# Attention followed by two squared-ReLU MLPs on one core: second-layer weight units issued a unit behind, first products in three banks, sums before remainders

## Chip, cores and metric

The kernel runs on one core of a Trainium2 chip. The metric is the device time of one execution in microseconds (us), the median of several runs.

## The reference, cut to what matters

```python
x = attention(q, k, v)            # 4 x 8 heads x 576 x 64: 4 heads local, 4 strided; scale 1/8
x = x.transpose(0, 2, 1, 3).reshape(2304, 512)
for w_in, w_out in (moe, moe2):   # [512, 2048], [2048, 512]
    r = np.maximum(x @ w_in, 0.0)
    x = (r * r) @ w_out
```

The weights are float64: a weight arrives as two 32-bit words, and the kernel first makes a float32 value of them.

## The kernel before, in words

Every float32 product is split: an operand is kept as a high part (rounded to fp32r) and a remainder (value minus high part), and a product is three matmuls, high by high, high by remainder, remainder by high.

**Blocks and steps.** The 2304 tokens make five blocks in each layer. Layer 1 is blocks 0 to 4: blocks 0, 1, 2 and 4 have 512 tokens and 16 steps each, block 3 has 256 tokens and 8 steps, each step being one or two of the 16 pieces (128 columns) of the hidden dimension. Block 5 is the 256 tokens of layer 2, 8 steps. A step of the main loop (lines 1500 to 1542) issues `mm1` of the next step (line 966) and then `mm2` of its own (line 1014). `mm1` fills a PSUM tile `ps_h` (24 narrow or 12 wide matmuls); ScalarE then evacuates it in three instructions, `r` (line 1001, ReLU), `sq` (1006) and `gh` (1007), and VectorE makes the remainder `gl` (1011). `mm2` of the step needs `gh` and `gl`. Blocks 6 to 9 (the other 2048 tokens of layer 2) use a seven-product scheme, one `frame` (line 1265) for each pair of pieces, 8 pairs per block.

**Banks of the first product.** `mm1` takes its tile from the pool `ps_h` (one bank), except that line 974 chooses `ps_a` (three banks) when `n_att[0] == len(att)`. The list `att` of attention work ends with entries that hold no operation; `att_to` is never called beyond `att_end[-1]`, the end of the last entry that holds one, so `n_att[0]` stays below `len(att)`.

**Second-layer weights.** While blocks 3 to 5 run, the weights of layer 2 are prepared in a list of units, `conv2` (lines 428 to 436), nine for a pair of pieces and 144 in all. There are eight pairs of the outer weights first, then eight pairs of the inner weights. In every step there are eight places (`point`, line 1508), three inside `mm1`, one behind its evacuation, four in and behind `mm2`; each adds `PACE` = 0.65 to a credit, and each whole credit issues one unit. They begin at the first step of block 3. The order of one pair i is: `start2(i)`, `sums_3(i-2)`, `start2(i+1)`, `whole2(i)`, `whole2(i+1)`, `rest2(i)`, `rest2(i+1)`, `sums_1(i)`, `sums_2(i)`.

- `start2`: two VectorE instructions on the raw words (lines 242, 246), then a ScalarE scaling of the result (263).
- `whole2`: VectorE joins the words (268), then ScalarE writes the high part (362).
- `rest2`: VectorE subtracts (371). For outer weights the second `rest2` of a pair stores both pieces, 1 MB, to DRAM (374).
- `sums_1`, `sums_2`: four VectorE sums of halves (382), then ScalarE writes their high parts in one instruction (414). For outer weights the target is `ops_out(4, 4)`, one buffer for all pairs.
- `sums_3`: VectorE subtracts the remainders (382); for outer weights a load of the next piece and a 1 MB store of that buffer follow (423).

All DMAs are issued from one queue (SP), and each engine executes its instructions in the order in which they are issued.

**A frame.** TensorE fills `ps_m` by `visit` (line 1220) with two products; ScalarE copies it to `m` (line 1308, shown in the trace as tile `u`); VectorE adds the halves of `m` (`u2`, line 1315) and, after the next `visit`, `a11` (line 1323, tile `r`). Before `m` stands, on ScalarE, the copy `ah` of sums `s13` that VectorE makes at the head of the frame (1297); behind it stands `bh` (1310). VectorE makes `bl` (1311), `u2`, and `work[0]` (a sum for x of the next block, line 1317), in that order, ahead of `a11`. In the first frame of blocks 7, 8 and 9 four sums of the block before (`heads`) come ahead of `s13`. In the last frame of a block `early` (a copy and a remainder of x) comes ahead of `m`. The second `visit` of the frame may write the bank only when `a11` has read it. Between the visits stand `gaps`, products of the current pair.

Of the kernel before, what the change touches and what calls it, by code (L numbers as in the profile page):

```python
# [14 lines left out]
ALU = mybir.AluOpType  # L15
# [40 lines left out]
SHIFT = (0, 4, 0)  # L56


XALL = 6 * 4 * 512 + 80
AT_V, AT_XN = P + 2 * P + 126, P + 2 * P + 126 + 5 * 260  # L60
OTHERS = AT_XN + 256 + 64

PACE = 0.65
N_WARM = 8
ZEROS = (0, 0, 0, 0, 0, 2, 2, 2, 2, 4, 4, 4)

# [103 lines left out]
def tile_attention_then_two_mlps(  # L170
# [69 lines left out]
    def sign_and_end(n):  # L240
        lower, upper = words(n)
        nc.vector.tensor_scalar(
            out=lower, in0=lower, scalar1=29, scalar2=None, op0=ALU.logical_shift_right
        )
        if n >= N_SIGNS:
            nc.vector.scalar_tensor_tensor(  # L246
                out=lower, in0=upper, scalar=-(2 ** 31), in1=lower, op0=ALU.bitwise_and, op1=ALU.bitwise_or
            )
# [102 lines left out]
        else:  # L351
            w_nat[i] = ops_out(f % 2 * 2, 2)

    def start2(i):
        sign_and_end(half1 + i)
        exponent_range(half1 + i)

    def whole2(i):
        together(half1 + i)
        natural(i)  # L360
        v = val[half1 + i].rearrange("p (h m) -> p h m", h=2)
        nc.scalar.activation(out=w_nat[i][:, :, 0], in_=v, func=AF.Copy)
        if i < NF and i % 2 == 0:
            load2("out")

    done2 = set()

# [31 lines left out]
    def sums_2(i):  # L399
        s = s_sum[i]  # L400
        v0, v1 = values_of(i)
        if i < NF:
            tt(s[:, 1], v1[:, 1], s[:, 0], ALU.subtract)
            tt(s[:, 3], s[:, 1], v1[:, 0], ALU.subtract)
            w = ops_out(4, 4)
            s_parts[i] = w[:, :, 0], w[:, :, 1]
        else:
            tt(s[:, 1], s[:, 0], v0[:, 0], ALU.subtract)
            tt(s[:, 3], v0[:, 1], s[:, 1], ALU.subtract)
            s_parts[i] = [  # L410
                wpool.tile([P, 4, HALF], F32R, tag=slot("out", i % NF + a), name="s")
                for a in range(2)
            ]
        nc.scalar.activation(out=s_parts[i][0], in_=s, func=AF.Copy)
        for n in (i, i + 1):
            del val[half1 + n]

    def sums_3(i):
        h, lo = s_parts[i]
        tt(lo, s_sum.pop(i), r32(h), ALU.subtract)  # L420
        if i < NF:
# [3 lines left out]
                in_=r32(xall[:, units_at + 4 * U:units_at + 8 * U]),  # L425
            )

    conv2 = []
    for i in range(0, half2 + 2, 2):
        if i < half2:  # L430
            conv2.append((start2, i))
        if i:
            conv2.append((sums_3, i - 2))
        if i < half2:
            conv2 += [(start2, i + 1), (whole2, i), (whole2, i + 1), (rest2, i), (rest2, i + 1)]
            conv2 += [(sums_1, i), (sums_2, i)]

    def conv2_by(n):
        while n and n_conv2[0] < len(conv2):
            fn, i = conv2[n_conv2[0]]  # L440
            kind, _, f = piece2(i)
            if f >= n_load2[kind]:
                return
            fn(i)
            n_conv2[0] += 1
            n -= 1

# [518 lines left out]
    def mm1(s, point):  # L966

        if s >= len(steps):
            return
        k, f = steps[s]  # L970
        ne = tiles_of(k)
        n = TB // ne
        x_hi, x_lo = block_x(k)
        if s != 1 and n_att[0] == len(att):
            ps = ps_a.tile([P, TB], F32, tag="a", name="ps_h")
        elif s != 1:
            ps = ps_h.tile([P, TB], F32, tag="h", name="ps_h")
        else:
            ps = ps_a.tile([P, TB], F32, tag="a", name="ps_h")
        for c in range(KC):  # L980
            for e in range(ne):
                w = ready2(f + e) if k == NB else ready(("in", 0, f + e))
                for i, (a, x) in enumerate(((0, x_hi), (0, x_lo), (1, x_hi))):

                    last = c == KC - 1 and i == 2 and e == ne - 1
                    product(
                        ps[:, e * n:(e + 1) * n],
                        lhsT=w[:, c // 2, a, c % 2 * P:(c % 2 + 1) * P] if k == NB
                        else w[:, a, c * P:(c + 1) * P],
                        rhs=x[:, c] if k == NB else x[:, c, x_at(n):x_at(n) + n],  # L990
                        start=c == 0 and e == 0 and i == 0,
                        stop=last,
                        halves=last and k == NB - 1 and f == 0,
                    )
                    one_small()
            if c < KC - 1:
                point()
        g0 = 48 if ne > 1 and blocks[k][0] == 0 else 0
        r = gpool.tile([P, TB], F32, tag="r", name="r", bufs=1)
        sq = gpool.tile([P, TB], F32, tag="sq", name="sq", bufs=1)  # L1000
        nc.scalar.activation(out=r, in_=ps, func=AF.Relu, scale=W_BACK)  # L1001
        h = gpool.tile([P, TB + P], F32R, tag="gh", name="gh", bufs=2)[:, g0:g0 + TB]
        lo = gpool.tile([P, 3 * HALF], F32R, tag="gl", name="gl", bufs=2)[:, g0:g0 + TB]
        if 0 < n_load[0] - n_part[0] or 0 < n_conv2[0] < len(conv2):

            nc.scalar.activation(out=sq, in_=r, func=AF.Square)
            nc.scalar.activation(out=h, in_=sq, func=AF.Copy)  # L1007
        else:
            nc.scalar.activation(out=h, in_=r, func=AF.Square)
            nc.vector.tensor_tensor(out=sq, in0=r, in1=r, op=ALU.mult)  # L1010
        nc.vector.tensor_tensor(out=lo, in0=sq, in1=r32(h), op=ALU.subtract)  # L1011
        gh[s], gl[s] = h, lo
# [252 lines left out]
    def frame(gaps, nxt, cur, heads=(), copy=None, early=None, work=None, late=()):  # L1265
# [16 lines left out]
        if cur:  # L1282
            s13, s24 = (
                gpool.tile([P, TB + P], F32, tag="gh", name="s", bufs=2)[:, :TB].rearrange(
                    "p (i n) -> p i n", i=2)
                for _ in range(2)
            )
            nc.scalar.activation(out=ah[:, 2], in_=a12, func=AF.Copy)
            if heads:
                for one in heads[:2]:  # L1290
                    one()
                tt(al[:, 2], a12, r32(ah[:, 2]), ALU.subtract)
                for one in heads[2:]:
                    one()
            tt(s13[:, 0], a21, a22, ALU.add)
            tt(s13[:, 1], a11, a21, ALU.subtract)
            nc.scalar.activation(out=ah[:, 0:2], in_=s13, func=AF.Copy)  # L1297
            if not heads:
                tt(al[:, 2], a12, r32(ah[:, 2]), ALU.subtract)
            tt(s24[:, 0], s13[:, 0], a11, ALU.subtract)  # L1300
            tt(s24[:, 1], a12, s24[:, 0], ALU.subtract)
            tt(al[:, 0:2], s13, r32(ah[:, 0:2]), ALU.subtract)
        if early is not None:
            early()
        ps = ps_h.tile([P, TB], F32, tag="h", name="ps_m")
        visit(k, q, ps, ("11", 0), ("s2", 1))
        m, u = (vpool.tile([P, 512], F32, tag="val", name="u") for _ in range(2))
        nc.scalar.activation(out=m, in_=ps, func=AF.Copy, scale=W_BACK)  # L1308
        if cur:
            nc.scalar.activation(out=bh[:, 2:4], in_=s24, func=AF.Copy)  # L1310
            tt(bl[:, 2:4], s24, r32(bh[:, 2:4]), ALU.subtract)

        u2, u3 = m[:, HT:], u[:, HT:]
        u4 = u[:, :HT]
        tt(u2, m[:, :HT], m[:, HT:], ALU.add)
        if work is not None:
            work[0]()
        for one in gaps[0]:
            one()
        if copy is not None:  # L1320
            copy()
        visit(k, q, ps, ("12", 2))
        add(a11, ps[:, :HT], m[:, :HT])
        nc.scalar.activation(out=a11, in_=a11, func=AF.Relu)
        nc.scalar.activation(out=a11, in_=a11, func=AF.Square)
        parts(bh[:, 0], bl[:, 0], a11)
# [149 lines left out]
    with tc.manual_schedule():  # L1476
# [23 lines left out]
        for s in range(len(steps)):  # L1500
# [7 lines left out]
            def point(s=s, layer=layer, j=j, f=f):  # L1508
                n_pt[0] += 1
                at = N_PT * s + n_pt[0]  # L1510
                for b, (p0, p1) in enumerate(spans):
                    if at > p0:
                        lo, hi = att_end[b], att_end[b + 1]
                        if b == 0 and at < LATE * N_PT:
                            hi = lo + (hi - lo) * EARLY // 100
                            p1 = LATE * N_PT
                        elif b == 0:
                            lo += (hi - lo) * EARLY // 100
                            p0 = LATE * N_PT
                        att_to(min(hi, lo + -(-(hi - lo) * (at - p0) // (p1 - p0))))  # L1520
                if n_part[0] < half1:
                    conv_by(1)
                elif k >= NB - 2:
                    credit[0] += PACE
                    while credit[0] >= 1.0:
                        conv2_by(1)
                        credit[0] -= 1.0
# [53 lines left out]
```

## Time and profile before

| | |
|---|---|
| median of 3 runs | 970.28 us (968.94 to 971.01) |
| the profiled execution | 971.93 us |
| its span, first to last instruction | 970.2 us |
| TensorE matmul busy | 892.5 us, 92% |
| VectorE busy | 688.2 us, 71% |
| ScalarE busy | 524.7 us, 54% |
| GpSimd busy | 17.7 us, 2% |
| granted clock of TensorE, mean | 0.984 |

The profile is that of one execution. Matmuls are pipelined and their ends are modelled, so TensorE busy at 92% does not mean that it works at its peak; what it waits for is read from its waits. Blocks 3 to 5 lie from about 367 us to 597 us of the span, the frames from about 600 us to the end.

### The profile page before, as it was taken

Reading aid. Unit: us, or ns where it says so; the run is one execution under the profiler, and the core shown is the slowest. Engines: PE = TensorE matmul, PEld = TensorE weight load, DVE = VectorE, ACT = ScalarE, POOL = GpSimd, SP = SyncE. Lnnn points to the kernel's source line nnn. Section 1 sums busy time; section 2 is a strip of 40 time slices with the busy share of each in tenths; the row PEclk is TensorE's granted clock in tenths of the full one; section 3 lists DMA queues with packets and bytes.
Section 4 is the critical chain, followed back from the end, with each engine's and each line's share of the span. In section 5 each row is a group of like instructions: output and inputs, shape, how many; then the busy total and the mean of one; then the engine's idle time right before and its main releaser. Section 6 shows DMA issues by size and latency. Waiting matters only on the chain. (4 is left out here: it accounts for less than half of the span.)

```text
span 970.2 us, 16096 instructions
## 1 busy us (share of the span) xinstructions
PE 892.5 (92%) x5719; PEld 791.9 (82%) x5719; DVE 688.2 (71%) x1742; ACT 524.7 (54%) x1204; POOL 17.7 (2%) x15
## 2 busy tenths in 40 slices
PE   9899999999999998877887879999899989998998
PEld 8788888887888888866666768988798889888998
DVE  6898974787677744665676665777767777777766
ACT  6877864676666644455555553444444444444442
POOL 0700000000000000000000000000000000000000
PEclk9999999999999999999999989999999999998999
DMA  8955411222222105676943264655665566555653
GB/s 266 347 176 194 147 40 68 87 73 80 86 76 63 54 1 191 232 251 243 338 133 105 87 254 163 199 171 160 184 212 173 153 217 189 160 164 165 193 177 128
DMA packets 81247, 155.21 MB, mean 160 GB/s; under 512 B 7440, under 2 KB 36240, under 8 KB 78096
## 3 DMA queue, kind: packets, MB, share of 16 engines
q1 hardware_dynamic: 81168, 154.19, 48.6%
q8 instruction: 45, 0.74, 0.3%
q14 instruction: 34, 0.28, 0.1%
HBM read 127.95 MB, written 26.21 MB: 159 GB/s over the span
## 5 line engine op out<-in xcount | busy, mean ns | idle before, releaser
L958 PE MATMUL ps_h<-xall,w 128*128 128x512 f32 (+1 forms) x1153 | 257.6, 368 | 38.6 <-ACT r L1001 38.6
L958 PEld LDWEIGHTS ps_h<-xall,w 128*128 128x128 f32 x1153 | 190.8, 195 | 71.8 <-ACT r L1001 45.4
L958 PE MATMUL ps_y<-gh,w 128*128 128x512 f32 (+1 forms) x640 | 156.4, 375 | 3.7 <-ACT o L1056 3.1
L958 PEld LDWEIGHTS ps_y<-gh,w 128*128 128x128 f32 x640 | 108.1, 188 | 21.1 <-ACT o L1056 3.5
L1226 PE MATMUL ps_m<-xall,s 128*128 128x256 f32 x768 | 111.0, 288 | 12.9 <-DVE r L1069 6.7
L1226 PEld LDWEIGHTS ps_m<-xall,s 128*128 128x128 f32 x768 | 97.5, 192 | 21.8 <-DVE r L1069 11.1
L1011 DVE TENSOR_TENSOR gl<-sq,gh 128x512 fp32r<-128x512 f32 x80 | 55.4, 692 | 67.7 <-ACT gh L1007 63.3
L1226 PE MATMUL ps_m<-xall,w 128*128 128x256 f32 x576 | 87.6, 289 | 10.5 <-ACT u L1308 10.1
L1253 PE MATMUL ps_y<-w,bh 128*128 128x256 f32 x496 | 94.6, 284 | 0.0
L1226 PEld LDWEIGHTS ps_m<-xall,w 128*128 128x128 f32 x576 | 75.1, 191 | 17.2 <-ACT u L1308 17.2
L958 PE MATMUL ps_y<-gl,w 128*128 128x512 f32 (+1 forms) x324 | 84.0, 370 | 0.0
L1001 ACT ACTIVATE r<-ps_h 128x512 f32<-128x512 f32 x80 | 47.2, 590 | 60.6 <-PE ps_h L958 52.0
L382 DVE TENSOR_TENSOR bl<-r,bh 128x256 fp32r<-128x256 f32 x64 | 27.2, 425 | 72.0 <-ACT bh L1065 44.4
L1253 PEld LDWEIGHTS ps_y<-w,bh 128*128 128x128 f32 x496 | 77.8, 193 | 0.0
L1253 PE MATMUL ps_y<-w,ah 128*128 128x256 f32 x372 | 72.0, 283 | 0.0
L1253 PE MATMUL ps_y<-w,bl 128*128 128x256 f32 x248 | 70.4, 284 | 0.0
L958 PEld LDWEIGHTS ps_y<-gl,w 128*128 128x128 f32 x324 | 55.8, 188 | 9.6 <-DVE gl L1011 0.4
L1010 DVE TENSOR_TENSOR sq<-r 128x512 f32<-128x512 f32 x38 | 26.3, 691 | 52.0 <-ACT r L1001 52.0
L1253 PEld LDWEIGHTS ps_y<-w,ah 128*128 128x128 f32 x372 | 58.0, 192 | 0.0
L1253 PE MATMUL ps_y<-w,al 128*128 128x256 f32 x186 | 52.7, 283 | 0.0
L263 ACT ACTIVATE raw<-raw 128x512 f32<-128x512 f32 x49 | 33.0, 673 | 36.4 <-DVE raw L246 36.4
L663 ACT ACTIVATE s<-s,m 96x128 f32<-96x128 f32 (+2 forms) x88 | 34.3, 390 | 33.4 <-DVE m L547 32.7
(121 smaller groups left out, 1497.0 us busy)
## 6 DMA issues: line engine op xcount, KB each, us to landing
w<-w_mem SPq DMA_DIRECT2D x221, 256.0 KB, 2.7
raw<-moe_w_in_d SPq DMA_DIRECT2D x32, 512.0 KB, 5.7
w_mem<-xall SPq DMA_DIRECT2D x16, 1024.0 KB, 5.4
raw<-moe_w_out_d SPq DMA_DIRECT2D x24, 512.0 KB, 4.6
xall<-w_mem SPq DMA_DIRECT2D x8, 1024.0 KB, 5.6
qk<-loc_qk_d SPq DMA_DIRECT2D x12, 416.0 KB, 3.1
out_d<-o SPq DMA_DIRECT2D x17, 256.0 KB, 3.5
y_dram<-o SPq DMA_DIRECT2D x16, 256.0 KB, 2.1
```

Source lines behind the costliest of these rows:

```text
L263: nc.scalar.activation(out=upper, in_=upper, func=AF.Copy, scale=2.0 ** (W_EXP // 8 - 112))
L382: nc.vector.tensor_tensor(out=out, in0=in0, in1=in1, op=op)
L663: nc.scalar.activation(out=blk, in_=blk, func=AF.Exp, scale=-1.0, bias=m[:nq, j:j + 1], accum_out=dens[i][:nq, j:j + 1],)
L958: nc.tensor.matmul(y[:, c:c + w], lhsT=lhsT, rhs=rhs[:, c:c + w], start=start and c == 0, stop=stop and c + w == n,)
L1001: nc.scalar.activation(out=r, in_=ps, func=AF.Relu, scale=W_BACK)
L1010: nc.vector.tensor_tensor(out=sq, in0=r, in1=r, op=ALU.mult)
L1011: nc.vector.tensor_tensor(out=lo, in0=sq, in1=r32(h), op=ALU.subtract)
L1226: nc.tensor.matmul(ps[:, half * HT:(half + 1) * HT], lhsT=w[:, j * P:(j + 1) * P], rhs=x[:, j], start=half == 0 and j == 0 and m == 0, sto ...
L1253: nc.tensor.matmul(banks[name][:, t * HALF:(t + 1) * HALF], lhsT=g[:, rows], rhs=w, start=first and t == 0 and m == 0, stop=end and t == 1 ...
```

## The change

Units of `conv2` become lists: `start2` is split into `sign2` (VectorE) and `range2` (ScalarE), `whole2` loses its ScalarE part to `high2`, `sums_2` loses its ScalarE part to `high_s`, and each ScalarE part is issued in the unit after the one with the VectorE part that it reads. There are 145 units. `PACE` becomes 0.72, and the units begin at the third step of block 3 (`START_2` = 4). `mm1` uses the pool of three banks once `n_att[0] >= att_end[-1]`. In a frame `ah` is issued behind `m`, `u2` ahead of `al` and `bl`, `early` behind `bl`, and `work[0]` behind `a11`. The tile `xall` is 32 columns shorter.

```diff
--- before.py
+++ after.py
@@ -56,11 +56,11 @@
 SHIFT = (0, 4, 0)
 
 
-XALL = 6 * 4 * 512 + 80
+XALL = 6 * 4 * 512 + 48
 AT_V, AT_XN = P + 2 * P + 126, P + 2 * P + 126 + 5 * 260
 OTHERS = AT_XN + 256 + 64
 
-PACE = 0.65
+PACE, START_2 = 0.72, 4
 N_WARM = 8
 ZEROS = (0, 0, 0, 0, 0, 2, 2, 2, 2, 4, 4, 4)
 
@@ -351,17 +351,21 @@
         else:
             w_nat[i] = ops_out(f % 2 * 2, 2)
 
-    def start2(i):
+    def sign2(i):
         sign_and_end(half1 + i)
+
+    def range2(i):
         exponent_range(half1 + i)
 
     def whole2(i):
         together(half1 + i)
+        if i < NF and i % 2 == 0:
+            load2("out")
+
+    def high2(i):
         natural(i)
         v = val[half1 + i].rearrange("p (h m) -> p h m", h=2)
         nc.scalar.activation(out=w_nat[i][:, :, 0], in_=v, func=AF.Copy)
-        if i < NF and i % 2 == 0:
-            load2("out")
 
     done2 = set()
 
@@ -411,9 +415,9 @@
                 wpool.tile([P, 4, HALF], F32R, tag=slot("out", i % NF + a), name="s")
                 for a in range(2)
             ]
-        nc.scalar.activation(out=s_parts[i][0], in_=s, func=AF.Copy)
-        for n in (i, i + 1):
-            del val[half1 + n]
+
+    def high_s(i):
+        nc.scalar.activation(out=s_parts[i][0], in_=s_sum[i], func=AF.Copy)
 
     def sums_3(i):
         h, lo = s_parts[i]
@@ -425,23 +429,30 @@
                 in_=r32(xall[:, units_at + 4 * U:units_at + 8 * U]),
             )
 
+
     conv2 = []
     for i in range(0, half2 + 2, 2):
-        if i < half2:
-            conv2.append((start2, i))
-        if i:
-            conv2.append((sums_3, i - 2))
-        if i < half2:
-            conv2 += [(start2, i + 1), (whole2, i), (whole2, i + 1), (rest2, i), (rest2, i + 1)]
-            conv2 += [(sums_1, i), (sums_2, i)]
+        old, new = i > 0, i < half2
+        if new:
+            conv2 += [[(sign2, i)], [(sign2, i + 1), (range2, i)]]
+        conv2.append([(sums_3, i - 2)] * old + [(range2, i + 1)] * new)
+        if new:
+            conv2 += [
+                [(whole2, i)],
+                [(whole2, i + 1), (high2, i)],
+                [(sums_1, i), (high2, i + 1)],
+                [(sums_2, i)],
+                [(rest2, i), (high_s, i)],
+                [(rest2, i + 1)],
+            ]
 
     def conv2_by(n):
         while n and n_conv2[0] < len(conv2):
-            fn, i = conv2[n_conv2[0]]
-            kind, _, f = piece2(i)
-            if f >= n_load2[kind]:
-                return
-            fn(i)
+            for fn, i in conv2[n_conv2[0]]:
+                if i % NF >= n_load2[piece2(i)[0]]:
+                    return
+            for fn, i in conv2[n_conv2[0]]:
+                fn(i)
             n_conv2[0] += 1
             n -= 1
 
@@ -971,7 +982,7 @@
         ne = tiles_of(k)
         n = TB // ne
         x_hi, x_lo = block_x(k)
-        if s != 1 and n_att[0] == len(att):
+        if s != 1 and n_att[0] >= att_end[-1]:
             ps = ps_a.tile([P, TB], F32, tag="a", name="ps_h")
         elif s != 1:
             ps = ps_h.tile([P, TB], F32, tag="h", name="ps_h")
@@ -1294,33 +1305,34 @@
                     one()
             tt(s13[:, 0], a21, a22, ALU.add)
             tt(s13[:, 1], a11, a21, ALU.subtract)
-            nc.scalar.activation(out=ah[:, 0:2], in_=s13, func=AF.Copy)
             if not heads:
                 tt(al[:, 2], a12, r32(ah[:, 2]), ALU.subtract)
             tt(s24[:, 0], s13[:, 0], a11, ALU.subtract)
             tt(s24[:, 1], a12, s24[:, 0], ALU.subtract)
-            tt(al[:, 0:2], s13, r32(ah[:, 0:2]), ALU.subtract)
-        if early is not None:
-            early()
         ps = ps_h.tile([P, TB], F32, tag="h", name="ps_m")
         visit(k, q, ps, ("11", 0), ("s2", 1))
         m, u = (vpool.tile([P, 512], F32, tag="val", name="u") for _ in range(2))
+
+        u2, u3 = m[:, HT:], u[:, HT:]
+        u4 = u[:, :HT]
         nc.scalar.activation(out=m, in_=ps, func=AF.Copy, scale=W_BACK)
         if cur:
+            nc.scalar.activation(out=ah[:, 0:2], in_=s13, func=AF.Copy)
             nc.scalar.activation(out=bh[:, 2:4], in_=s24, func=AF.Copy)
+        tt(u2, m[:, :HT], m[:, HT:], ALU.add)
+        if cur:
+            tt(al[:, 0:2], s13, r32(ah[:, 0:2]), ALU.subtract)
             tt(bl[:, 2:4], s24, r32(bh[:, 2:4]), ALU.subtract)
-
-        u2, u3 = m[:, HT:], u[:, HT:]
-        u4 = u[:, :HT]
-        tt(u2, m[:, :HT], m[:, HT:], ALU.add)
-        if work is not None:
-            work[0]()
+        if early is not None:
+            early()
         for one in gaps[0]:
             one()
         if copy is not None:
             copy()
         visit(k, q, ps, ("12", 2))
         add(a11, ps[:, :HT], m[:, :HT])
+        if work is not None:
+            work[0]()
         nc.scalar.activation(out=a11, in_=a11, func=AF.Relu)
         nc.scalar.activation(out=a11, in_=a11, func=AF.Square)
         parts(bh[:, 0], bl[:, 0], a11)
@@ -1520,7 +1532,7 @@
                         att_to(min(hi, lo + -(-(hi - lo) * (at - p0) // (p1 - p0))))
                 if n_part[0] < half1:
                     conv_by(1)
-                elif k >= NB - 2:
+                elif (k, f) >= (NB - 2, START_2):
                     credit[0] += PACE
                     while credit[0] >= 1.0:
                         conv2_by(1)
```

## Rows read from the trace of the kernel before

**Rows 1.** The page, part 1: busy time, share of span and instructions of each engine.

```profile
PE 892.5 (92%) x5719; PEld 791.9 (82%) x5719; DVE 688.2 (71%) x1742; ACT 524.7 (54%) x1204; POOL 17.7 (2%) x15
```

**Rows 2.** Waits of TensorE, 372 to 600 us: waited for, us in total, times, longest.

```profile
PE ps_h L958 <- ACT r L1001: 38.6, 21, 4.1
```

**Rows 3.** Waits of TensorE, 600 to 970 us, the frames.

```profile
PE ps_m L1226 <- ACT u L1308: 10.1, 7, 2.7
PE ps_m L1226 <- DVE r L1069: 6.7, 12, 0.6
PE ps_m L1226 <- DVE u L1069: 6.2, 19, 0.7
```

**Rows 4.** Waits of VectorE, 360 to 600 us.

```profile
DVE gl L1011 <- ACT gh L1007: 58.3, 28, 5.0
```

**Rows 5.** Timeline 442 to 449 us: start, duration, engine, line; in brackets idle before.

```profile
442.98 1.23 DVE L382 TENSOR_TENSOR xall<-raw,xall 128x1024 fp32r<-128x1024 f32 x1
444.12 0.42 DVE L242 TENSOR_SCALAR others<-others 128x512 int32<-128x512 int32 x1
444.58 0.69 DVE L246 SCALAR_TENSOR_TENSOR others<-others 128x512 int32<-128x512 int32 x1
445.19 0.69 DVE L268 SCALAR_TENSOR_TENSOR val<-others 128x512 int32<-128x512 int32 x1
...
445.91 0.63 ACT L362 ACTIVATE xall<-val 128x512 fp32r<-128x512 f32 x1
446.44 0.58 ACT L1001 ACTIVATE r<-ps_h 128x512 f32<-128x512 f32 x1
...
447.71 0.63 ACT L1007 ACTIVATE gh<-sq 128x512 fp32r<-128x512 f32 x1
448.38 0.69 DVE L1011 TENSOR_TENSOR gl<-sq,gh 128x512 fp32r<-128x512 f32 x1 [2.51 <-ACT gh L1007]
```

**Rows 6.** Timeline of ScalarE, line 1001: first of block 3, then blocks 4 and 5.

```profile
367.08 0.60 ACT L1001 ACTIVATE r<-ps_h 128x512 f32<-128x512 f32 x1 [4.20 <-PE ps_h L958]
...
481.64 0.57 ACT L1001 ACTIVATE r<-ps_h 128x512 f32<-128x512 f32 x1
...
547.36 0.58 ACT L1001 ACTIVATE r<-ps_h 128x512 f32<-128x512 f32 x1
...
591.30 0.60 ACT L1001 ACTIVATE r<-ps_h 128x512 f32<-128x512 f32 x1 [1.04 <-PE ps_h L958]
596.75 0.60 ACT L1001 ACTIVATE r<-ps_h 128x512 f32<-128x512 f32 x1 [4.19 <-PE ps_h L958]
```

**Rows 7.** Timeline of ScalarE, line 414: first and last of the eight outer pairs.

```profile
387.55 1.06 ACT L414 ACTIVATE xall<-raw 128x1024 fp32r<-128x1024 f32 x1 [1.55 <-DVE raw L382]
...
477.65 1.06 ACT L414 ACTIVATE xall<-others 128x1024 fp32r<-128x1024 f32 x1 [2.22 <-DVE others L382]
```

**Rows 8.** The stores of line 374 (first) and of line 423 (second), eight each.

```profile
DMA to landing us min/median/max: 3.8/4.6/8.0
...
DMA to landing us min/median/max: 5.1/6.4/6.5
```

**Rows 9.** Timeline of three frames: plain, with work[0], with heads.

```profile
619.55 0.84 PE L1226 MATMUL ps_m<-xall,s 128*128 128x256 f32 x6
...
620.84 0.58 ACT L1308 ACTIVATE u<-ps_m 128x512 f32<-128x512 f32 x1
...
622.98 0.42 DVE L1069 SCALAR_TENSOR_TENSOR r<-ps_m,u 128x256 f32<-128x256 f32 x1
...
623.45 0.39 PE L1226 MATMUL ps_m<-xall,s 128*128 128x256 f32 x1
...
668.82 0.86 PE L1226 MATMUL ps_m<-xall,s 128*128 128x256 f32 x5 [0.55 <-DVE r L1069]
...
702.64 1.17 PE L1226 MATMUL ps_m<-xall,w 128*128 128x256 f32 x6 [2.75 <-ACT u L1308]
```

**Rows 10.** Busy time by engine, 446.4 to 547.4 us, 14 steps of block 4; PEclk is granted.

```profile
446.40:547.40 101.00, 81.48 (x350) 64.26 (x350) 69.38 (x123) 55.28 (x89) 0.00 (x0) 0.98 0.53 182
```

## The prediction

> **What bounds the kernel now.** I read the engines' busy times first: TensorE is busy for 92% of the span [rows 1], so at most some 78 us of the 970 can go without taking matmuls away, and only what TensorE waits for matters. Its waits by stretch come next. In blocks 3 to 5 it waits 38.6 us, in 21 stalls, for `r` to free the one `ps_h` bank [rows 2]. In the frames it waits 10.1 us for the copy `m` (seven stalls), 6.7 us for `a11` (twelve, at most 0.6) and 6.2 us for later sums [rows 3].
>
> Why `r` is late is read from VectorE, which waits 58.3 us in 28 stalls in front of `gl` [rows 4]: 2.1 us each. One step shows the loop [rows 5]: VectorE ends a unit at 445.88, ScalarE does that unit's own copy at 445.91, then `r`, `sq` and `gh` until 448.34, and only then `gl` runs, after 2.51 us of nothing on VectorE. So the two engines wait for each other once a step, and TensorE for both: 14 steps of block 4 take 100.9 us (446.44 to 547.36) [rows 5, 6], 7.21 each, with VectorE busy for 69% [rows 10]; a step with no units takes 5.45 us (591.30 to 596.75) [rows 6].
>
> **The change, term 1: a step with units.** Starts on VectorE follow each other after 0.46 us (a 0.42 instruction), 0.61 (a 0.69) and 1.14 (a 1.23) [rows 5]. The nine units of a pair hold two pairs of sign instructions (2 x 1.07), two joins and two remainders (4 x 0.61), four short sums (about 1.5 together) and `sums_3` (1.14): 7.2 us, 0.80 per unit. The step then is units, `gl` (0.61), and the wait in front of `gl`. I count that wait for each of the nine places where `gl` can fall, as the chain of 2.5 us (2.9 behind the wide copy) less the VectorE work issued since the result that the last ScalarE copy reads. Old order: 2.52, 1.38, 2.52, 2.49, 2.49, 1.89, 1.28, 0.60, 2.91, mean 2.0, as measured (2.1). New order, in which that result is always one unit older: 0.64, 1.45, 1.38, 0.77, 1.88, 1.82, 1.02, 2.31, 1.71, mean 1.44. Old step: 5.2 x 0.80 + 0.61 + 2.0 = 6.8, where 7.21 is measured. New step, with 0.72 x 8 = 5.76 units: 4.6 + 0.61 + 1.44 = 6.65; of the 0.4 that the count misses I carry half: 6.85, between 6.65 and 7.05.
>
> So the wait shrinks but stays. The banks do not remove it, since bank and TensorE are not in this loop; they let TensorE run a step ahead, so that its stall moves from `r` to `gh`, and uneven steps no longer add up.
>
> **Term 2: the store behind the wide copy.** `high_s` overwrites the one buffer that `sums_3` of the pair before has stored. That store lands 5.1 to 6.5 us after its issue, mostly 6.4; the store of line 374 takes 4.6, at most 8.0 [rows 8]. Before, seven units lay between the two, at least 8 us; now four (0.61 + 0.61 + 0.67 + 0.80 = 2.7 us and at most one `gl`). So ScalarE will stand at `high_s` for the DMA in most outer pairs, with `r` queued behind it, VectorE's `gl` behind that, and TensorE's `mm2` last. The loop of a pair is: from `high_s` to the end of the next `sums_3` 7.4, 6.8, 5.7 or 5.2 us when `gl` falls in between (four places of the 5.76), else 2.2, mean 5.0; 0.45 to issue the load and the store; 6.4 to land: 11.85 us, against 9 / 5.76 x 6.85 = 10.7 for VectorE alone. Before, the eight outer pairs took 12.9 each (387.55 to 477.65 by seven) [rows 7].
>
> Replayed with the credit's own places for `gl` (behind units 2, 7, 13, 19, 25, 30, 36 ...): block 3's first `r` is at 367.08 [rows 6], three steps of 5.6 bring the first units to 384, the first `high_s` to 391.6 and the eighth to 474.3. `r` of block 4's step 7 follows at 475.3, where it was at 481.64 [rows 6]: 6.3 us ahead, though with 74 units left instead of 70. The last three outer pairs share the DMA engines with the loads of the inner weights; I take off 1 us for each: **3.3 us gained** at this point.
>
> **Term 3: inner weights.** No store here. Nine steps to block 5 take 65.7 us now (481.64 to 547.36) [rows 6], then 9 x 6.85 = 61.7: 4.0. Block 5 takes 49.4 us (547.36 to 596.75), 4.3 of its seven intervals with units, so 2.7 x 5.45 = 14.7 and 8.1 for each of the others. With 3.85 such steps, each 0.36 shorter: 0.45 x 2.65 + 3.85 x 0.36 = 2.6. **6.6 us.**
>
> **Term 4: frames.** In a plain frame `ps_m` is complete at 620.39 and `m` starts at 620.84, behind `ah`, which waits for `s13` [rows 9]. With `m` first it starts at 620.43; `ah` and `bh` follow to 622.16, `bl` to 622.8, and `a11` starts at 622.84 instead of 622.98: 0.15 us in each of 13 frames, 2.0. In the twelve with `work[0]` the stall of 0.55 goes too [rows 3, 9]: `work[0]` then fits into the 1.4 us in which VectorE waits for ReLU, square and copy of `a11`. 12 x (0.55 + 0.2) = 9.0. With `early` the stall for `m` goes, and `a11` comes as late as before: 0. In the three first frames the 2.75 us for `m` [rows 9] only move: `a11` still waits behind four sums and `s24`, and comes about 0.6 us earlier with the same stall in front of the next `visit`: 0.5 each, 1.5. **12.5 us**, between 6 and 18. XALL and the loads are costed at nothing: the loads of raw words are issued two pairs ahead, and land 5 us later.
>
> **Sum.** 3.3 + 6.6 + 12.5 = 22.4. The profiled execution took 971.9 us, so 949.5; it stands 1.65 above the median, so **948 us**.
>
> The Trainium skill (DMA: Bandwidth & Descriptors, Anatomy of one DMA, fitted on GpSimd's queue) gives about 2.0 us plus the bytes at 436 GB/s, an estimate of 4.4 us for 1 MB. By it the pair's loop would be 9.9 us, VectorE would lead, and the sum would be that of the first rival below; the row of 6.4 us, behind a load in the same queue, speaks against it.
>
> **Rivals.**
> - *The store is hidden after all*: it lands in 4.6 us, as line 374's does [rows 8]. Then outer pairs take 10.7, seven of them give 8 us more: 940. For it: 4.6 is the nearest row of the same size. Against: a 512 KB load is issued just ahead. Chance 0.20.
> - *Blocks 3 to 5 give nothing*: waits on the store and a step that stays near 7.2 with more units in it eat terms 2 and 3, and the frames alone remain: 959. For it: the old count missed 0.4 us a step. Chance 0.20.
> - *The store wait turns the sign*: each of the seven pairs must lose 22.4 / 7 = 3.2 us more, so the store must land after 9.6 us, where the longest row is 8.0. At 10 us: 7 x 3.6 = 25, so 973. TensorE, idle for 4 us and more at a time, would add slow matmuls. Chance 0.06.
> - *TensorE's clock*: it now stalls in nearly every step. At the level of 1.2 GHz throughout, a step would take 10.9 instead of 6.85, and 25 such steps 101 us: 1050. Against: in 14 steps with such stalls the granted clock was 0.98 [rows 10]. Chance 0.02. The Trainium skill (TensorE: Matmul & The Clock Gate, A second HAM failure mode) states just this danger for cycling through PSUM banks with small idle times between groups; no row here bears it out.
> - *Nothing moves*: the same waits under other names, 970. Chance 0.04.
>
> **How the numbers follow.** The forecast holds 0.48, with its own range from 943 to 955. The range of 8 in 10 takes in the hidden store (940, less 4 if frames give 18) and the empty blocks (959, and 965 if the frames give 6): 936 to 965. A measurement of this kernel can tell about 0.2%, 1.9 us, from no change. Faster by more: 0.48 + 0.20 + 0.20 = 0.88; slower 0.06 + 0.02 = 0.08; same 0.04.
>
> **What would show it.** ScalarE's waits on line 414's successor name the DMA of `w_mem`, 2 to 4 us in most outer pairs. TensorE's waits for `r` all but vanish, and waits of `mm2` for `gh` take their place. VectorE's stalls before `gl` fall from 2.1 to about 1.4 us among inner weights. Block 5's last `r` comes near 587 instead of 596.75. In the frames the waits for `a11` at 0.55 go, those for `m` shrink to next to nothing, and three stalls of 2 to 3 us stay in the first frames, now for `a11`. The prediction is wrong if the outer pairs' `high_s` wait for VectorE alone, or if steps among the inner weights stay at 7.2.

## The result and the profile after

The changed kernel takes 947.48 us (median of 4 runs, 945.62 to 947.84) against 969.72 us for the kernel before in the same measurement: a ratio of 0.9766, interval 0.9748 to 0.9783. The forecast was 948 us. The profiled execution took 947.56 us, with a span of 945.8 us, 24.4 us less than the 970.2 before.

Busy times first (the page, part 1). TensorE has the same 5719 matmuls as in [rows 1] and is busy 11.4 us less, so its listed waits hold only part of the gain; 8.5 us of this lie in the frames, whose busy time follows below.

```profile
PE 881.1 (93%) x5719; PEld 784.4 (83%) x5719; DVE 685.6 (72%) x1745; ACT 521.2 (55%) x1201; POOL 17.7 (2%) x15
```

The frames before and after (busy time by engine; PEclk, the granted clock, is the third column from the right):

```profile
596.75:970.20 373.45, 346.00 (x2720) 329.42 (x2718) 269.51 (x575) 163.34 (x350) 0.00 (x0) 0.98 0.56 174
586.26:945.80 359.54, 337.49 (x2720) 325.79 (x2718) 266.71 (x575) 162.43 (x350) 0.00 (x0) 0.99 0.57 181
```

The waits of TensorE in 360 to 575 us (waited for, us in total, times, longest) answer to [rows 2]. The 38.6 us for `r` are gone; 18.1 us for `gh` stand in their place, and one wait of 6.5 us for a DMA has grown from 3.1.

```profile
PE ps_y L969 <- ACT gh L1018: 18.1, 12, 4.7
PE ps_y L1113 <- DMA xall<-w_mem: 6.5, 1, 6.5
PE ps_y L969 <- ACT o L1067: 6.3, 3, 3.7
```

The same view of the frames, 572 to 970 us, answers to [rows 3]. No wait for the copy `m` is left; `a11` (line 1080, tile r) now has seven waits of 9.5 us in all instead of twelve of 6.7.

```profile
PE ps_m L1237 <- DVE r L1080: 9.5, 7, 2.4
PE ps_m L1237 <- DVE u L1080: 5.4, 16, 0.7
PE ps_m L1237 <- ACT r L1349: 1.2, 3, 0.4
```

VectorE's waits in front of `gl` are 50.5 us in 24 stalls in 360 to 600 us, against 58.3 in 28 [rows 4]. The nine among the inner weights, 478 to 540 us, come to 13.7 us; the nine before, in 482 to 548 us, came to 17.9, or 2.0 each.

```profile
DVE gl L1022 <- ACT gh L1018: 13.7, 9, 4.6
```

```profile
DVE gl L1011 <- ACT gh L1007: 17.9, 9, 2.9
```

The first of the nine after is the 4.6 us. It stands behind the last wide copy of an outer pair, which itself waited for a store (at 477.25 below); the other eight are 1.1 us each.

```profile
480.14 0.69 DVE L1022 TENSOR_TENSOR gl<-sq,gh 128x512 fp32r<-128x512 f32 x1 [4.63 <-ACT gh L1018]
```

ScalarE has a wait that was not there before (its waits, 360 to 600 us): the wide copy of a pair's sums, line 420, stands for the store of the pair before, six times, 21.9 us. The stores that it waits for are those of line 427, whose times from issue to landing follow; they are as in [rows 8], with a longest of 8.6.

```profile
ACT xall L420 <- DMA w_mem<-xall: 21.9, 6, 5.0
```

```profile
DMA to landing us min/median/max: 5.0/6.4/8.6
```

Where the time came from is read from the line of `r` (now 1012), which answers to [rows 6], and from the wide copy, which answers to [rows 7].

```profile
366.80 0.60 ACT L1012 ACTIVATE r<-ps_h 128x512 f32<-128x512 f32 x1 [4.20 <-PE ps_h L969]
...
390.39 1.05 ACT L420 ACTIVATE xall<-raw 128x1024 fp32r<-128x1024 f32 x1
...
402.60 1.06 ACT L420 ACTIVATE xall<-others 128x1024 fp32r<-128x1024 f32 x1 [3.53 <-DMA w_mem<-xall]
...
477.25 1.06 ACT L420 ACTIVATE xall<-others 128x1024 fp32r<-128x1024 f32 x1 [3.25 <-DMA w_mem<-xall]
478.21 0.58 ACT L1012 ACTIVATE r<-ps_h 128x512 f32<-128x512 f32 x1
...
539.11 0.58 ACT L1012 ACTIVATE r<-ps_h 128x512 f32<-128x512 f32 x1
...
586.26 0.60 ACT L1012 ACTIVATE r<-ps_h 128x512 f32<-128x512 f32 x1 [3.70 <-PE ps_h L969]
```

From these rows, and the same instructions before:

| stretch | before | after | gained | forecast |
|---|---|---|---|---|
| start to `r` of block 4, step 7 | 481.64 | 478.21 | 3.4 | 3.3 |
| from there to the first `r` of block 5 | 65.72 | 60.90 | 4.8 | 4.0 |
| from there to the last `r` of block 5 | 49.39 | 47.15 | 2.2 | 2.6 |
| from there to the end (frames) | 373.45 | 359.54 | 13.9 | 12.5 |
| sum | 970.2 | 945.8 | 24.4 | 22.4 |

### The profile page after: what moved, and what is told of

Its sections match the earlier page's. It is cut to its first block, busy times and chain, and to the rows that moved or that the text cites. A ratio compares the mean times of both kernels' runs of the same rounds, so it can differ in the third digit from the quotient of the medians.

```text
span 945.8 us, 16062 instructions
## 1 busy us (share of the span) xinstructions
PE 881.1 (93%) x5719; PEld 784.4 (83%) x5719; DVE 685.6 (72%) x1745; ACT 521.2 (55%) x1201; POOL 17.7 (2%) x15
## 4 chain that ended last, share of the span: by engine, by line
PE 58%; DVE 21%; ACT 11%; DMA 7%; issue 3%; SPq 0%; DVEq 0%; ACTq 0%
PE ps_h L969 15%; PE ps_y L969 14%; PE ps_m L1237 13%; PE ps_y L1264 7%; DMA w_mem<-xall 3%; DVE s L386 3%; DVE r L1080 2%; DVE bl L386 2%; PE ps_s L626 2%; DVE xall L386 2%; PE ps_x L702 2%; DVE gl L1022 2%; PE ps_pt L758 1%; ACT sq L1017 1%; ACT gh L1018 1%
## 5 line engine op out<-in xcount | busy, mean ns | idle before, releaser
L969 PE MATMUL ps_h<-xall,w 128*128 128x512 f32 (+1 forms) x1153 | 247.4, 358 | 0.0
L969 PEld LDWEIGHTS ps_h<-xall,w 128*128 128x128 f32 x1153 | 185.5, 189 | 26.2
L969 PE MATMUL ps_y<-gh,w 128*128 128x512 f32 (+1 forms) x640 | 162.8, 386 | 25.3 <-ACT gh L1018 18.8
L1237 PE MATMUL ps_m<-xall,s 128*128 128x256 f32 x768 | 113.5, 292 | 18.0 <-DVE r L1080 9.5
L1237 PE MATMUL ps_m<-xall,w 128*128 128x256 f32 x576 | 82.7, 279 | 0.0
L1021 DVE TENSOR_TENSOR sq<-r 128x512 f32<-128x512 f32 x41 | 28.3, 691 | 58.2 <-ACT r L1012 58.2
L1299 ACT ACTIVATE ah<-c 128x256 fp32r<-128x256 f32 x31 | 13.0, 418 | 69.0 <-DVE c L1246 68.8
```

Source lines behind the costliest of these rows:

```text
L969: nc.tensor.matmul(y[:, c:c + w], lhsT=lhsT, rhs=rhs[:, c:c + w], start=start and c == 0, stop=stop and c + w == n,)
L1237: nc.tensor.matmul(ps[:, half * HT:(half + 1) * HT], lhsT=w[:, j * P:(j + 1) * P], rhs=x[:, j], start=half == 0 and j == 0 and m == 0, sto ...
```

## The experiments

The theory on trial: blocks 3 to 5 are set by a loop of VectorE and ScalarE through `gl` and by the store behind the wide copy, not by the bank of the first product; the frames gain by themselves. The rivals give the blocks' gain to the banks (B), the frames' gain to what lies ahead of them (F), or hold that the wait for the store is filled with other work anyway (H), or that the store is slow by itself. Intervals are of the ratio to the kernel before on the same chip.

**One bank in the changed kernel.**

```diff
-        if s != 1 and n_att[0] >= att_end[-1]:
+        if s != 1 and n_att[0] == len(att):
```

> The changed kernel with the first product back in its one bank; units, pace and frames as changed. Theory L (the loop of VectorE and ScalarE through gl, and the store, set blocks 3 to 5; the bank is not in that loop): the last r of block 5 comes 0 to 3 us later than the 586 us of the changed kernel, total 947 to 951 us; TensorE's waits move back from gh to r and from 18 us to about 30, without lengthening the steps. Rival B (the three banks carry the gain of blocks 3 to 5, since TensorE waited 38.6 us for r before): the 10 us of blocks 3 to 5 go, total 955 to 960 us.

Measured: 948.92 us (946.81 to 949.96), ratio 0.978, interval 0.9753 to 0.9807: not to be told from the changed kernel's 0.9766. The waits of TensorE in 365 to 600 us are back on `r`, and larger than the 18.1 for `gh`, yet the steps are the same: `r` of block 4's step 7 at 477.93 and the first of block 5 at 538.82, where the changed kernel has 478.21 and 539.11.

```profile
PE ps_h L969 <- ACT r L1012: 25.2, 15, 4.5
```

```profile
477.93 0.58 ACT L1012 ACTIVATE r<-ps_h 128x512 f32<-128x512 f32 x1
538.82 0.58 ACT L1012 ACTIVATE r<-ps_h 128x512 f32<-128x512 f32 x1
```

So in the changed kernel the bank is in no loop that sets these steps. TensorE waits under one name or another for engines that set the pace without it. Only the last `r` comes later, at 588.60 instead of 586.26, in the bare steps behind the last unit. Rival B falls.

**The banks alone.** The line of `mm1`, in the kernel before.

```diff
-        if s != 1 and n_att[0] == len(att):
+        if s != 1 and n_att[0] >= att_end[-1]:
```

> The kernel before with the three banks alone. Theory L: the stalls of TensorE for r (38.6 us) take the name gh, steps among units stay at 7.0 to 7.2 us, total 966 to 970 us. Rival B: steps shrink towards the 5.5 us of TensorE, total 945 to 960 us.

Measured: 967.63 us (964.59 to 970.54), ratio 0.9971, interval 0.9952 to 0.999. The steps of block 4 stay where they were (`r` at 445.54 and 546.51, 7.21 apart for 14), and 25.2 of the 38.6 us of waits changed their name:

```profile
PE ps_y L958 <- ACT gh L1007: 25.2, 15, 2.5
PE ps_y L958 <- ACT o L1056: 7.2, 2, 4.5
PE ps_y L1102 <- DMA xall<-w_mem: 4.3, 1, 4.3
```

The 38.6 us of [rows 2] were thus a symptom: three banks are worth about 3 us by themselves, gained in the last steps of block 5 (last `r` at 592.9 instead of 596.75).

**The frames alone.** The part of the diff that lies in `frame`, all of it, in the kernel before.

```diff
-            nc.scalar.activation(out=ah[:, 0:2], in_=s13, func=AF.Copy)
...
-        if work is not None:
-            work[0]()
...
         add(a11, ps[:, :HT], m[:, :HT])
+        if work is not None:
+            work[0]()
```

> The kernel before with the new order in the frames alone. Term 4 of the prediction (12.5 us; between the traces of before and after the frames gave 13.9 us): 970 - 13 = 957 us, 955 to 959. Rival F (the frames' gain comes in part from TensorE's clock or from what blocks 3 to 5 leave behind): 960 to 966 us.

Measured: 957.69 us (954.21 to 958.25), ratio 0.9869, interval 0.9839 to 0.99, or 12.7 us. As the theory has it. The part of F on what blocks 3 to 5 leave behind falls, since they are unchanged in this run (last `r` at 596.95). The part on the clock is met by single frames at full clock, in the section on the prediction.

**The units alone.** The diff without the line of `mm1` and without `frame`, so `ps_h` keeps its one bank.

```diff
-PACE = 0.65
+PACE, START_2 = 0.72, 4
...
-    def start2(i):
+    def sign2(i):
...
+    def high_s(i):
+        nc.scalar.activation(out=s_parts[i][0], in_=s_sum[i], func=AF.Copy)
```

> The kernel before with the new units, pace and start alone, one bank, old frames. Theory L: nearly the whole 10 us of blocks 3 to 5, total 959 to 963 us. Rival B: 967 us or more, since without banks TensorE still stalls for r.

Measured: 962.01 us (961.41 to 965.58), ratio 0.9929, interval 0.9904 to 0.9955, or 6.9 us, within theory L's 959 to 963; rival B's 967 falls. The last `r` comes at 587.08. By the ratios the three parts alone are 0.9971, 0.9869 and 0.9929: in us of 970, 2.8 + 12.7 + 6.9 = 22.4, where the whole change gives 22.7 by its ratio. They add up. Within this part the later start and the split of the units were not tried one by one; the pace is tried below.

**The wide copy two units later.** The first sign unit of the next pair takes it, in the changed kernel.

```diff
-            conv2 += [[(sign2, i)], [(sign2, i + 1), (range2, i)]]
+            conv2 += [[(high_s, i - 2)] * old + [(sign2, i)], [(sign2, i + 1), (range2, i)]]
...
-                [(rest2, i), (high_s, i)],
+                [(rest2, i)],
```

> The changed kernel with the wide copy of a pair's sums (high_s) issued two units later, with the first sign unit of the next pair. Theory S (ScalarE stands at that copy for the store of the pair before, 22 us in six waits, and the queue behind it pays): the waits of line 420 for the DMA fall to under 5 us, an outer pair takes 10.7 to 11.2 us instead of 12.4, the last r of block 5 comes near 577 to 580, total 939 to 943 us. Rival H (the wait is filled by VectorE's other units and costs nothing): 946 to 949 us.

Measured: 934.23 us (932.87 to 935.98), ratio 0.9622, interval 0.959 to 0.9655: 13 us below the changed kernel, more than expected, and not in the way I expected. The copy still waits for the store, five times:

```profile
ACT xall L420 <- DMA w_mem<-xall: 14.4, 5, 3.4
```

The reason is in the loop, not in the distance to the store. From one copy to the next the loop is the way from the copy to `sums_3`, the issue and the landing. Issued later, the copy is two units from `sums_3` instead of four, so less stands between the two: from a copy to the issue of its pair's store (line 427) the first seven pairs take 4.5 us on average instead of 5.4. The landing is the same (median 6.4), and the copies come 11.7 us apart (402.75 to 472.93 by six) instead of 12.4 (402.60 to 477.25). My expectation had compared only what lies between the store and the next copy. The `r` of block 4's step 7 comes 8.6 us sooner: 4.3 are the eighth copy's, the other 4.3 come with `r` standing ahead of that copy instead of behind it.

```profile
469.60 0.58 ACT L1014 ACTIVATE r<-ps_h 128x512 f32<-128x512 f32 x1
472.93 1.06 ACT L420 ACTIVATE xall<-others 128x1024 fp32r<-128x1024 f32 x1 [1.43 <-DMA w_mem<-xall]
```

H falls, but this run does not price the wait: 7.5 us less of it came with 13 us, and among the inner weights, where there is no store, the nine steps take 59.1 us instead of 60.9, and block 5 45.1 instead of 47.15. What shortens those steps was not tried. The run with the store ahead of the load, below, changes the wait with the copy in its place.

**The slower pace.** In the changed kernel:

```diff
-PACE, START_2 = 0.72, 4
+PACE, START_2 = 0.65, 4
```

> The changed kernel with PACE back at 0.65. By my count of a step (units x 0.80, gl 0.61, wait 1.44) each step with units costs only 2.05 us beyond its units and TensorE's 5.45 us run beside them, so units spread over more steps are cheaper: 27.9 steps instead of 25.2 carry units and 2.7 bare steps of 5.45 turn into 2.05: 8 to 10 us less, 937 to 941 us. Rival P (a higher pace is what shortened these blocks): 951 to 956 us.

Measured: 944.53 us (943.59 to 945.4), ratio 0.9732, interval 0.9707 to 0.9756: 3 us less than the changed kernel, and the two intervals just overlap; neither the 8 to 10 nor rival P. To the first `r` of block 5 the count of steps held: 529.45 against 539.11, 9.7 us ahead. But that lead is work put off: 22 steps of eight places with 0.07 less credit are some twelve units, at the counted 0.80 us each. Block 5 gave 5.9 back (529.45 to 582.44, 53.0 us against 47.15): the last units now lie among its x sums, and TensorE waits 3.3 us for a weight itself (waits of TensorE, 540 to 590 us; the 6.3 for the DMA stand in the changed kernel too).

```profile
PE ps_y L1113 <- DMA xall<-w_mem: 6.3, 1, 6.3
PE ps_h L969 <- DVE w L375: 3.3, 1, 3.3
```

So the higher pace is no gain of its own. It buys earlier weights for block 5, and pays for them in block 4.

**Both.** The diffs of the two runs before, together.

> Both edits, the later copy and PACE 0.65. If the store and the count of steps are both right they add in part: outer pairs 11 us, 27.9 steps of 6.4 with units, last r near 568 to 573, total 930 to 936 us. If the store alone or the pace alone sets the time, no better than the better of the two single edits.

Measured: 933.29 us (930.39 to 936.56), ratio 0.9617, interval 0.9584 to 0.965: the same as the later copy alone, within the intervals. The time fits both cases of the expectation: 930 to 936 holds the later copy's 934 as well, so it does not tell them apart. Step 7 of block 4 has its `r` at 461.67 us, ahead of both single edits, and block 5 again gives most of the lead back (last `r` at 571.17 against 573.79).

**The sum behind `a11`, alone.** In the kernel before:

```diff
-        if work is not None:
-            work[0]()
         for one in gaps[0]:
...
         add(a11, ps[:, :HT], m[:, :HT])
+        if work is not None:
+            work[0]()
```

> The kernel before with work[0] moved behind a11 and nothing else. Term 4's split: the twelve stalls of 0.55 us for a11 go, 12 x 0.55 to 0.6 = 6.6 to 7.2 us, total 962 to 964 us, and the rest of the frames' gain (5 to 7 us) belongs to m ahead of ah. Rival (the sum delays the remainders behind a11 by its 0.6 us, and the wait moves to the later sums): 967 us or more.

Measured: 962.93 us (960.24 to 964.66), ratio 0.9927, interval 0.9905 to 0.9949, or 7.1 us. In the frames the waits for `a11` are gone, and the two others are those of [rows 3]:

```profile
PE ps_m L1226 <- ACT u L1308: 10.1, 7, 2.7
PE ps_m L1226 <- DVE u L1069: 6.3, 19, 0.7
```

The rest of the frames' 12.7 us, 5.6 by the difference of two medians, belongs to the other moves there; `m` ahead of `ah` was not tried alone.

**The store ahead of the load.** In `sums_3` of the changed kernel:

```diff
-            load2("out")
             nc.sync.dma_start(
                 out=w_mem[i // 2][:, 4 * U:8 * U],
...
+            load2("out")
```

> The changed kernel with sums_3 issuing its store ahead of the load of the next raw piece. Theory Q (the store of line 423 lands after 6.4 us where the other store of 1 MB takes 4.9, because 512 KB are queued ahead of it): it lands after 4.5 to 5.2 us, ScalarE's waits of line 420 for the DMA fall from 22 us to 10 to 14, seven pairs gain 1.2 to 1.6 us each, total 937 to 941 us. Rival (the landing time is the store's own, or the load that comes later makes VectorE wait for its raw words): 945 to 949 us.

Measured: 941.44 us (940.19 to 943.51), ratio 0.9711, interval 0.9688 to 0.9735: 5 to 6 us gained. The store lands 1.4 us sooner, and three waits of the copy are left:

```profile
DMA to landing us min/median/max: 4.9/5.0/6.3
```

```profile
ACT xall L420 <- DMA w_mem<-xall: 7.3, 3, 3.3
```

So 1.4 of the 6.4 us of landing in [rows 8] came from the 512 KB queued ahead of it. The order on the engines is that of the changed kernel here, so this run prices the wait: 14.6 us less of it gave 5.3 us at block 4's step 7 (`r` at 472.94 instead of 478.21). H, that it costs nothing, falls; but the larger part of the wait does not show in the time.

**Block 5's second weights a step earlier.** In the changed kernel:

```diff
-        narrow_w(q + 1)
+        if q:
+            narrow_w(q + 1)
...
                 narrow_w(0)
+                narrow_w(1)
```

> The changed kernel with the load of block 5's second weights (the 6.5 us wait of TensorE for the DMA in its second step) issued a step earlier. Theory: the x loads queued behind it land earlier too, VectorE's 4.6 us wait for them shrinks, total 943 to 945 us. Rival: the wait only moves to the x loads or to gl, 946 to 949 us.

Measured: 943.59 us (941.61 to 945.61), ratio 0.9722, interval 0.9691 to 0.9753, within what was expected. TensorE's wait for the second weights is gone; a wait of 4.3 us for the third stands in its place, a step later. What shrank as well is ScalarE's wait for the x loads (line 1076, from 4.1 to 1.2 us), and with it the loop: `r` of block 5's first to third steps are 16.3 us apart, 539.44 to 555.71, instead of 19.2, 539.11 to 558.31.

```profile
557.77 3.02 PE L1113 MATMUL ps_y<-xall,gh 128*128 128x512 f32 x8 [4.31 <-DMA xall<-w_mem]
```

**Together.** The later copy, the store ahead of the load, the earlier weights, and `early` behind `work[0]`.

```diff
-        if early is not None:
-            early()
         for one in gaps[0]:
...
             work[0]()
+        if early is not None:
+            early()
```

> The changed kernel with the copy two units later, the store ahead of the load, block 5's second weights loaded a step earlier, and early behind a11 in the last frame of a block (three stalls of 0.7 us). If each keeps most of what it gives alone: 934 - 4 (load) - 2 (early) - 3 to 6 (store) = 922 to 928 us. If the load and the store only compete for the same wait: 929 to 932 us.

Measured: 926.26 us (925.15 to 927.05), ratio 0.9552, interval 0.953 to 0.9573: faster than both kernels, 21 us below the changed one. ScalarE's waits for the store are down to 1.6 us in two stalls of line 420, with 3.1 us more in one of line 368. In the frames three waits for `a11` remain, those of the first frames of blocks 7 to 9 (waits of TensorE, 590 to 940 us):

```profile
PE ps_m L1240 <- DVE r L1082: 7.1, 3, 2.4
```

## Why the prediction was right, point by point

**The loop.** This was the reading that decided: the waits for `r` are the largest of TensorE in blocks 3 to 5, and they say nothing of the bank. The bank alone changed their name and gave 3 us; the units alone gave 7. A step among inner weights takes 60.90 / 9 = 6.77 us, forecast 6.85, but that closeness is in part luck: the first of the nine still pays for a store. The other eight take 6.59 us each (486.37 to 539.11), and the wait in front of `gl` is 1.1 us there, counted 1.44. So the wait was sized 0.3 us too long, and the 0.2 us carried for what the count misses was about right.

**The store.** The replay gave the first wide copy at 391.6 and the eighth at 474.3, with 3 us more for the loads that share the DMA engines; they came at 390.39 and 477.25. That the eighth falls where it should is luck. No row gave the 3 us, and they were booked on the last three pairs, which took 36.5 us, 1.1 more than by the replay's mean of 11.8 a pair; the four pairs before took 3.1 more, and the first copy came 1.2 sooner. The new wait has the place and the engine that term 2 gave it, and five of the six are within its 2 to 4 us; one is 5.0. The price of the first rival, 940 us for a store that lands in 4.6 us, is borne out by the run in which it lands after 5.0 us, at 941.4.

**Block 5.** 2.2 us for 2.6, though not in one piece: the first steps lost time on a DMA that the sum did not hold. With every step earlier, the load of the second weights still goes out only behind block 4's last stores, and TensorE waits 6.5 us for it where it waited 3.1. I had seen the wait of 3.1 us and left it out.

**The frames.** 13.9 us between the two traces and 12.7 us alone, forecast 12.5. The prices of single frames can be read from one copy `m` to the next, here four frames that answer to each other, before and after.

```profile
620.84 0.58 ACT L1308 ACTIVATE u<-ps_m 128x512 f32<-128x512 f32 x1
631.74 0.58 ACT L1308 ACTIVATE u<-ps_m 128x512 f32<-128x512 f32 x1
642.64 0.58 ACT L1308 ACTIVATE u<-ps_m 128x512 f32<-128x512 f32 x1
654.14 0.58 ACT L1308 ACTIVATE u<-ps_m 128x512 f32<-128x512 f32 x1
```

```profile
609.81 0.60 ACT L1318 ACTIVATE u<-ps_m 128x512 f32<-128x512 f32 x1 [0.60 <-PE ps_m L1237]
620.53 0.60 ACT L1318 ACTIVATE u<-ps_m 128x512 f32<-128x512 f32 x1 [0.57 <-PE ps_m L1237]
631.19 0.60 ACT L1318 ACTIVATE u<-ps_m 128x512 f32<-128x512 f32 x1 [0.55 <-PE ps_m L1237]
641.91 0.60 ACT L1318 ACTIVATE u<-ps_m 128x512 f32<-128x512 f32 x1 [0.56 <-PE ps_m L1237]
```

A plain frame took 10.90 us and takes 10.72, priced at 0.15 less; one with `work[0]` took 11.50 and takes 10.72 (10.87 with `work[0]` moved alone), priced at 0.75 less. The granted clock is 1.00 over both stretches, so these gains are not the clock's. The plain frame gains although the trace lists no wait there for `m` or `a11`; that fits a short wait counted as busy time, whose ends are modelled. By these frames, twelve with `work[0]` and thirteen plain ones make an estimated 11.7 of the 13.9 us. What the rise of the clock over all frames, from 0.98 to 0.99, gave was not separated. Of the split, 7.1 us were measured for `work[0]`, where the twelve stalls of 0.55 us were priced at 6.6. The three first frames still stall, 2.4 us each, now for `a11`, as forecast. In the last frames `early` stands ahead of `a11` and costs 0.7 us there; they were priced at 0 because the old stall for `m` goes, which was 0.5 us, so the two about cancel. One price in the rivals is a slip: with the frames alone the sum gives 970.3 - 12.5 = 958, not 959.

**TensorE's clock.** The rival did not come, but the clock is lower in these blocks. Over the nine inner steps it is 0.94, where it was 0.97, and in 360 to 600 us the lowest of the slices of 10 us has 0.53, where the lowest before had 0.68; four slices lie below 0.9 in both (busy time by engine, as above; the first line is that of the kernel before).

```profile
481.60:547.40 65.80, 52.80 (x230) 42.12 (x230) 44.87 (x80) 36.29 (x60) 0.00 (x0) 0.97 0.33 102
420.00:430.00 10.00, 5.04 (x12) 3.31 (x11) 4.36 (x10) 4.82 (x9) 0.00 (x0) 0.53 0.82 322
478.20:539.10 60.90, 53.82 (x241) 42.92 (x242) 48.74 (x88) 37.36 (x61) 0.00 (x0) 0.94 0.40 135
```

At 0.53 the clock is near its level of 1.2 GHz, at the end of block 3, where TensorE stalls three times for `o` (1.4, 1.3 and 3.7 us). What the slow matmuls cost was not tried by itself. The Trainium skill (TensorE: Matmul & The Clock Gate, A second HAM failure mode) names idle gaps from cycling banks as the danger. The two pairs of traces that differ in the bank alone point both ways: from the first `r` of block 3 to block 4's step 7 the clock is 0.94 with three banks and 0.97 with one in the old units, 0.94 and 0.92 in the new; and in the new the steps are the same to 0.3 us.

**What was wrong** lies in the expectations of two runs. The later copy was to end the wait for the store; the wait stayed and the loop became shorter. The slower pace was to give 8 to 10 us; it was 9.7 ahead at the end of block 4 and lost 5.9 in block 5, because the count treated every step as having only units beside it. What was not tried is a second buffer for the sums.

## What to carry to other kernels

The largest wait of the busiest engine names who was last, not what sets the pace: count the loop of the engines that wait for each other, and see whether the resource that you would add is in it. When an instruction is moved away from the result that it reads, count also what it moves towards, above all the DMA that must have left its target, and price that as a loop: copy, consumer, issue, landing, next copy. Where a load and a store are issued together, the one that something waits for goes first.

## What the runs showed of the hardware

A store of 1 MB landed 6.4 us after its issue with a load of 512 KB issued just ahead in the same queue, and 5.0 us with the load behind it (medians of eight); the one of line 378, with no load issued just ahead of it, took 4.9. The Trainium skill (DMA: Bandwidth & Descriptors, Anatomy of one DMA, fitted on GpSimd's queue) puts 1 MB at an estimate of 4.4 us; the traces agree with it within 0.6 us for a store with no load queued just ahead.
